# One training step on one core: program order on every engine, transposes moved into the forward part, one pass over w2 saved, output rows in V's space

## The chip, the cores and the metric

The kernel runs on one core of a Trainium2 chip. The metric is the device time of one execution in microseconds (us), lower is better; each time quoted is the median of several executions. An execution over 1.5% above the fastest of its kernel counts as slow. The notes called "the Trainium skill" are cited by page title and section where the argument rests on them.

Names: PE is TensorE (PEld its weight loads), DVE is VectorE, ACT is ScalarE, POOL is GpSimd, SP is SyncE. A tile is a piece of on-chip memory that the program allocates from a pool. PE's results go into tiles in PSUM, and DVE or ACT copy them from there to SBUF; such a copy of an output is called an eviction. A one-bank tile holds 512 values of 4 bytes, or 1024 of 2 bytes, in each partition (row of memory), and a two-bank tile twice that.

## The reference

A step of decoding with its backward pass, batch and sequence length 1, in bfloat16:

```python
x = x + attention(layernorm(x), K, V, wq, wo)   # A1: 32 heads, 4 kv heads of 128, last 4096 of 32768 positions
x = x + mlp(layernorm(x), w1, b1, w2)           # B2: 1024 -> 3584 (mish) -> 1024
x = x + attention(layernorm(x), K, V, wq, wo)   # A3: the same weights again
x = x + mlp(layernorm(x), w1, b1, w2)           # B4: the same weights again
out, vjp = jax.vjp(f, x, K, V, wq, wo, w1, b1, w2)
return out, *vjp(grad_out)
```

Matrices are multiplied with one column only, so every weight is read for one 128x1 product per 128x128 block. The backward needs the weights transposed, in blocks of 128x128, which PE does against an identity. The weight gradients are outer products, and the cache gradients (4 x 32768 x 128 each) are zero outside the last 4096 positions: 112 blocks of 0.5 MB of zeros must be written ("the zeros").

## The kernel before

The kernel streams weights in chunks of 0.5 MB. These are the parts that matter (cuts are marked with `# ...`).

```python
ctx.enter_context(tc.manual_schedule(engines={ET.SP}))  # only SP in program order; the scheduler orders the others
pt   = ctx.enter_context(tc.tile_pool(name="pt", bufs=4, space=PSUM))    # one-bank tiles
pbig = ctx.enter_context(tc.tile_pool(name="pbig", bufs=1, space=PSUM))
pacc = ctx.enter_context(tc.tile_pool(name="pacc", bufs=1, space=PSUM))

def xpose_unit(ap2d, nb):                       # 8 transposes, one PSUM tile of their own, one copy back in place
    ps = pt.tile([P, 8, P], BF16, name="tps", tag="pt")
    for b in range(nb):
        nc.tensor.transpose(ps[:, b, :], ap2d[:, b * P:(b + 1) * P], ident_bf[:])
    evac(ap2d, ps[:, 0:nb, :].rearrange("p b c -> p (b c)"), 0.08 * nb, 0.12 * nb)   # on DVE or ACT by load

# backward of w2, one chunk of 16 blocks (w1 and wo are alike)
    zeros(1)                                    # one 0.5 MB write of zeros beside each chunk
    for tt in range(2):
        xpose_unit(w[:, tt, :], 8)
    for tt in range(2):
        # ... 8 products 128x1 each

def xpose_resident():                           # V, K and wq stay in SBUF; all their transposes in one go, in A3's backward
    xpose_kv(V_t); xpose_kv(K_t)
    # ... wq

# outputs: each weight gradient brings its vectors into rows by small DMAs, then outer products
def rows_put(R, side, kind, groups):
    rt = to_rows(...)                           # one of 4 buffers "rt"
    for q, off, b0, nb, step in groups:
        for lay in range(2):
            nc.gpsimd.dma_start(R[...], rt[...])        # 80 such row copies in the whole kernel, 0.5 to 2 KB each
R = new_rows("R2"); rows_put(...); dw_tall(R, ...)      # w2, then b1, w1, wo, kv, wq in the same way
# ... four outer products of 512 columns into places of one bank (six in rotation), four evictions of 512
nc.gpsimd.dma_start(out_7.rearrange("(c p t) -> p c t", p=P, t=2), db1_bf[:]...)   # b1's gradient, 7 KB in 4-byte pieces
```

## Time and profile before

Three executions gave 726.65 us in the median (723.12 to 728.49).

| | before |
|---|---|
| span of the profiled execution | 723.6 us |
| bytes moved | 197.29 MB, 273 GB/s |
| PE busy | 470.8 us (65%) |
| mean granted clock | 0.569 |

This is the page of the kernel before, its second part: the span in 40 equal slices of 18.1 us. A digit is the busy share in tenths; PEclk is the granted clock in tenths of full speed; DMA is the share of the 16 DMA engines, and GB/s what they moved.

```profile
PE   3564334563367788988987766778675464878364
...
PEclk9985555555565555757965555555555555555555
DMA  8999999449989999994006999999503646567547
GB/s 317 418 415 408 292 335 372 180 160 326 342 283 396 341 364 374 387 301 167 3 3 240 394 218 354 384 339 346 229 3 151 259 166 242 231 269 249 184 169 296
```

DMA is nearly full almost everywhere up to slice 30, with three holes: A3's forward (slices 8 and 9), the resident transposes and A3's attention (slices 19 to 21), and A1's attention (slices 29 and 30). The last ten slices are the outputs, where DMA is about half busy. The clock is at 0.5 for most of the span.

The next view is the table of stretches: window, then busy time and count of instructions of each engine, granted clock, DMA share, GB/s. The windows are the backward of B4's w2, of B4's w1, the resident transposes, and the outputs.

```profile
core 0: us, PE busy (x) PEld busy (x) DVE busy (x) ACT busy (x) POOL busy (x), PEclk, DMA share, GB/s
208.00:248.00 40.00, 31.15 (x441) 27.28 (x441) 12.19 (x20) 11.13 (x11) 0.65 (x1) 0.59 0.95 346
248.00:292.00 44.00, 36.03 (x464) 31.09 (x465) 12.07 (x21) 12.61 (x15) 0.00 (x0) 0.50 1.00 369
330.00:361.40 31.40, 30.70 (x515) 30.61 (x514) 25.82 (x41) 23.70 (x26) 0.00 (x0) 0.92 0.15 55
540.00:723.60 183.60, 108.67 (x517) 36.18 (x516) 97.72 (x171) 90.80 (x166) 86.06 (x159) 0.50 0.58 218
```

The backward of w1 is at DMA share 1.00 although PE is busy for 36 of 44 us at clock 0.50: each 0.5 MB weight chunk carries a 0.5 MB zero write, so it is the transfers that set its pace. From 330 us DMA is nearly idle (share 0.15) while PE transposes, at clock 0.92, and DVE and ACT copy.

These are waits of PE by what ended them: microseconds in total, number of waits, longest. PE waits for copies (the `w_c` lines) when it multiplies with the transposed chunk.

```profile
PE acc L170 <- DMA w_c<-in_B_w_dram: 47.9, 52, 2.0
PE acc L170 <- ACT w_c L150: 20.3, 45, 0.8
...
PE acc L170 <- DVE w_c L147: 7.6, 34, 0.4
...
PE tps L155 <- DMA w_c<-in_B_w_dram: 5.8, 4, 3.8
```

The row copies land 1.5 to 3.4 us after their issue, most kinds at about 1.6. This line is from the list of DMA issues (count, size, median us from issue to landing):

```profile
Ro<-rt POOLq DMA_DIRECT2D x16, 2.0 KB, 1.6
```

### The profile page before, as it was taken

How to read it: one execution, taken by the hardware profiler on the slowest of the kernel's cores; microseconds unless marked ns; L12 is line 12 of the kernel's file. 1: busy time of each engine (PE TensorE's matmuls, PEld its weight loads, DVE VectorE, ACT ScalarE, POOL GpSimd, SP SyncE). 2: the span in 40 equal slices, each digit the busy share in tenths (PEclk: the TensorE clock that was granted, in tenths of full speed). 3: DMA queues.
4: the chain of work that ended last, by engine and by line, in shares of the span. 5: the costliest groups of instructions: out<-in, count | busy, mean ns of one | idle time of the engine just before them, and what ended most of it. 6: DMA issues, size and time to landing. Idle time of an engine off the chain costs nothing. (4 is left out here: it accounts for less than half of the span.)

```text
span 723.6 us, 16229 instructions
## 1 busy us (share of the span) xinstructions
PE 470.8 (65%) x7092; PEld 352.3 (49%) x7092; DVE 236.4 (33%) x468; ACT 199.8 (28%) x294; POOL 89.8 (12%) x173
## 2 busy tenths in 40 slices
PE   3564334563367788988987766778675464878364
PEld 2444334353356676868976655667461010135210
DVE  1140010200122322526823221222314454676255
ACT  0120000000012222425802222222104464665245
POOL 0000000000000000000000000000005555423462
PEclk9985555555565555757965555555555555555555
DMA  8999999449989999994006999999503646567547
GB/s 317 418 415 408 292 335 372 180 160 326 342 283 396 341 364 374 387 301 167 3 3 240 394 218 354 384 339 346 229 3 151 259 166 242 231 269 249 184 169 296
DMA packets 59751, 197.29 MB, mean 273 GB/s; under 512 B 12577, under 2 KB 12577, under 8 KB 58657
## 3 DMA queue, kind: packets, MB, share of 16 engines
q1 hardware_dynamic: 46800, 156.27, 59.7%
q0 software_dynamic: 12880, 40.00, 14.8%
q8 instruction: 55, 0.90, 0.5%
q14 instruction: 16, 0.12, 0.1%
HBM read 97.53 MB, written 98.58 MB: 271 GB/s over the span
## 5 line engine op out<-in xcount | busy, mean ns | idle before, releaser
L170 PEld LDWEIGHTS <-w_c 128*128 128x128 bf16 x1792 | 61.1, 105 | 106.6 <-DMA w_c<-in_B_w_dram 56.2
L150 ACT COPY w_c<-tps 128x1024 bf16<-128x1024 bf16 (+1 forms) x52 | 47.3, 909 | 163.0 <-PE tps L155 89.2
L147 DVE COPY w_c<-tps 128x1024 bf16<-128x1024 bf16 (+1 forms) x68 | 45.8, 677 | 127.0 <-PE tps L163 67.1
L163 PE MATMUL tps<-ident_bf,w_c 128*128 128x128 bf16 x448 | 52.9, 311 | 5.8 <-DMA w_c<-in_B_w_dram 5.8
L155 PE MATMUL tps<-ident_bf,w_c 128*128 128x128 bf16 x448 | 49.2, 296 | 5.8 <-DMA w_c<-in_B_w_dram 5.8
L163 PEld LDWEIGHTS <-w_c 128*128 128x128 bf16 x448 | 45.2, 144 | 5.9 <-DMA w_c<-in_B_w_dram 5.9
L155 PEld LDWEIGHTS <-w_c 128*128 128x128 bf16 x448 | 42.5, 138 | 6.2 <-DMA w_c<-in_B_w_dram 6.1
L155 PE MATMUL tps<-ident_bf,wo_c 128*128 128x128 bf16 x352 | 40.3, 307 | 0.0
L170 PEld LDWEIGHTS <-wo_c 128*128 128x128 bf16 x608 | 20.4, 105 | 36.8 <-DMA wo_c<-in_A_wo_dram 14.0
L155 PEld LDWEIGHTS <-wo_c 128*128 128x128 bf16 x352 | 35.0, 143 | 0.0
L170 PE MATMUL acc<-nB_pair,w_c 128*128 128x1 bf16 x448 | 16.7, 166 | 28.1 <-DMA w_c<-in_B_w_dram 25.0
L150 ACT CAST st_t<-ops 128x512 bf16<-128x512 f32 x43 | 24.2, 597 | 35.9 <-PE ops L170 31.1
L170 PE MATMUL acc<-a_pair,w_c 128*128 128x1 bf16 x448 | 16.2, 166 | 27.4 <-DMA w_c<-in_B_w_dram 23.0
L147 DVE COPY wo_c<-tps 128x1024 bf16<-128x1024 bf16 x26 | 18.0, 691 | 47.9 <-PE tps L155 47.4
L150 ACT COPY wo_c<-tps 128x1024 bf16<-128x1024 bf16 x18 | 18.2, 1012 | 51.6 <-PE tps L155 51.6
L147 DVE CAST st_t<-ops 128x512 bf16<-128x512 f32 x39 | 25.5, 684 | 20.6 <-PE ops L170 18.9
L170 PE MATMUL acc<-dh_pair,w_c 128*128 128x1 bf16 x448 | 21.5, 168 | 16.4 <-ACT w_c L150 11.2
L170 PE MATMUL acc<-gB_pair,w_c 128*128 128x1 bf16 x448 | 19.4, 167 | 12.9 <-ACT w_c L150 9.1
L170 PE MATMUL ops<-Rq 2*128 2x512 bf16 x42 | 17.2, 586 | 14.5 <-DMA Rq<-rt 13.4
L170 PE MATMUL ops<-Ro 2*128 2x512 bf16 x44 | 18.1, 587 | 10.8 <-DMA Ro<-rt 8.4
L170 PE MATMUL acc<-gA_pair,wo_c 128*128 128x1 bf16 x352 | 16.3, 168 | 13.2 <-ACT wo_c L150 10.2
L520 POOL DMA_DIRECT2D out_dram<-rt x2 | 1.2, 588 | 190.8 <-DVE rt L515 190.8
(545 smaller groups left out, 819.7 us busy)
## 6 DMA issues: line engine op xcount, KB each, us to landing
out_dram<-zt SPq DMA_DIRECT2D x112, 512.0 KB, 7.3
w_c<-in_B_w_dram SPq DMA_DIRECT2D x64, 448.0 KB, 5.3
w_c<-in_B_w_dram SPq DMA_DIRECT2D x52, 512.0 KB, 5.6
wo_c<-in_A_wo_dram SPq DMA_DIRECT2D x38, 512.0 KB, 6.6
out_dram<-st_t POOLq DMA_DIRECT2D x30, 512.0 KB, 3.6
out_dram<-st_kv POOLq DMA_DIRECT2D x16, 512.0 KB, 4.8
out_dram<-st_wq POOLq DMA_DIRECT2D x16, 512.0 KB, 3.7
K_163<-in_A_k_cache_dram SPq DMA_DIRECT2D x1, 1024.0 KB, 12.5
```

The source lines that it names most:

```text
L147: nc.vector.tensor_copy(out_ap, in_ap)
L150: nc.scalar.copy(out_ap, in_ap)
L155: nc.tensor.transpose(ps[:, b, :], ap2d[:, b * P:(b + 1) * P], ident_bf[:])
L163: nc.tensor.transpose(ps[:, b, :], ap2d[:, o:o + 2 * P - 1:2], ident_bf[:])
L170: nc.tensor.matmul(out_ap, lhsT=lhsT, rhs=rhs, start=start, stop=stop, skip_group_check=True, **kw)
L520: nc.gpsimd.dma_start(out_flat.rearrange("(n p) -> n p", p=P), rt[0:n, :])
```

## The change

Its intent is to take three holes out of the DMA's work. The resident blocks are transposed in the forward part, where PE has time between loads; B4's last forward pass over w2 also serves its backward, so ten w2 loads and a 40 us stage disappear; and V's space, free after the last attention, holds more output buffers, so that all row copies can be issued together and evictions be 1024 wide. The backward loops are software-pipelined by one chunk, and the order of the program is now the order on every engine. The diff, cut to its core (cuts marked `...`):

```diff
-    ctx.enter_context(tc.manual_schedule(engines={ET.SP}))
+    ctx.enter_context(tc.manual_schedule())
-    pt = ctx.enter_context(tc.tile_pool(name="pt", bufs=4, space=bass.MemoryType.PSUM))
-    pbig = ctx.enter_context(tc.tile_pool(name="pbig", bufs=1, space=bass.MemoryType.PSUM))
+    vpool = tc.alloc_tile_pool(name="vpool", bufs=1)
+    p2 = ctx.enter_context(tc.tile_pool(name="p2", bufs=3, space=bass.MemoryType.PSUM))
...
+    def psum2(shape, dtype, name):                       # a tile of two banks
+        t = p2.tile([P, 1024 if dtype == FP32 else 2048], dtype, name=name, tag="p2")
+        return shaped(t, shape)
+
+    def xpose2(halves):
+        ps = psum2([P, 16, P], BF16, "tps")
+        for i, (blocks, dst) in enumerate(halves):
+            for b, ap in enumerate(blocks):
+                nc.tensor.transpose(ps[:, 8 * i + b, :], ap, ident_bf[:])
+            n = len(blocks)
+            evac(dst, ps[:, 8 * i:8 * i + n, :].rearrange("p b c -> p (b c)"), 0.08 * n + 0.03, 0.11 * n + 0.15)
...
+    def pipe(items, T, M, lag=1):                        # transposes of chunk i, then products of chunk i-1
+        n = len(items)
+        for i in range(n + lag):
+            if i < n:
+                T(items[i])
+            if i >= lag:
+                M(items[i - lag], i - lag)
...
+            if g_bf is not None:                         # B4's w1 forward also transposes resident blocks
+                zeros(i % 2)
+                fill(2 if i % 2 else 1)
...
+            fwd_rows2(yacc, w, c, a_bf, c == 0, c == NW2 - 1)
+            if g_bf is not None:                         # B4's w2 forward also serves the backward
+                ...
+                xpose_rows2(w)
+                if held:
+                    bwd_rows2(dacc, held.pop(), c - 1, g_bf)
+                held.append(w)
...
+    def after_v():                                       # called in A1's backward, V is dead from there
+        vpool.release()
+        ...
+        rows["w2"] = new_rows("R2")
+        rows_put(rows["w2"], 0, "a", tall_groups(TF))
+        ...                                              # all eight row sets, 80 row copies
     zeros(1000)                                          # the 58 zero blocks left, without a wait, on SP
...
-                for q in range(4):
-                    ev_out(sts[q // 2][:, q % 2, i * 512:(i + 1) * 512], pss[q])
+            pss = [psum2([P, 1024], FP32, "ops") for _ in range(2)]
             for i in range(2):
+                for tt in range(2):
+                    b = 2 * c + tt
+                    outer(R, b % 4, (b // 4) * P, i * 512, pss[tt][:, i * 512:(i + 1) * 512])
+            for tt in range(2):
+                ev_out(st[:, tt, :], pss[tt][:])
```

## The prediction

> **What bounds it now.** Timeline and stage windows of the span (723.6 us) show three regimes.
> 1. Forward, 0 to 208 us: A1 and B2 (3 to 121 us) run at DMA share 0.95 to 1.01, 337 to 407 GB/s: bound by loads. A3 (121 to 163) is a latency chain, share 0.54.
> 2. Backward, 208 to 540 us. Streamed stages (208 to 330, 384 to 516) have DMA share 0.94 to 1.01, because each 0.5 MB weight chunk carries a 0.5 MB zero write; a chunk takes about 3.0 us. PE transposes, waits for the copy (0.3 to 0.8 us on ACT or DVE), multiplies; its granted clock is mostly 0.50 and 16 transposes take 1.87 us. From 330.9 to 361.4 PE only transposes resident V, K and wq (warm, 16 in 0.89 us) while DMA moves 55 GB/s; then comes attention (3 GB/s).
> 3. Output, 540 to 724 us: DMA share 0.58. 80 row copies issued by POOL, 0.52 us each, stall every matrix; 512-wide evictions take 0.684 us (DVE) and 0.597 us (ACT); four stage buffers.
>
> **What the change does.**
> - Removes the 30.5 us resident block; its 32 pairs of transposes go to A3's wo loop (8) and B4's w1 loop (24).
> - B4's w2 pass also serves the backward: the 40 us stage at 208 to 248 goes, B4's own w2 loop grows from about 21 to 30-35 us. 10 w2 and 6 wo chunk loads fewer (197 to about 189 MB).
> - Backward loops are pipelined by one chunk: PE no longer waits for copies. I expect the clock to rise to 0.8-1.0 there (dense stretch 294 to 300 us: 1.00). The Trainium skill, "TensorE: Matmul & The Clock Gate", Part 4, says transposes do not raise the clock; this trace disagrees (1.00 from 336 to 340 us, transposes alone).
> - Only about 54 of 112 zeros stay before the tail, 58 follow the last wo load. Backward chunks fall to 1.3-2.0 us.
> - Output: 1024-wide evictions (estimate from the 512-wide ones: 1.22 and 1.03 us, so 1.13 us per engine and chunk instead of 1.28), nine stage buffers, all row copies together (41 us of POOL) ahead of the first output write, partly under A1's backward.
>
> **Sum (end of stage, us).** A1+B2: 115 (was 121). A3: 162. B4 w1 with 24 fills: 198. w2 double pass: 232. w1 backward: 258. wo backward: 286. A3 attention backward: 308 (was 384). B2 w2: 334; w1: 360. A1 wo: 383; attention: 410 (was 540). Tail: row copies hold the first output write until about 450, while the 58 zeros (30 MB, 78 us) drain; then 69 of 78 chunks at about 1.5 us: 555 to 565. DMA alone from about 372 us: 70 MB at 380 GB/s is 185 us, giving 557; both limits agree.
>
> Prediction: 570 us, range 542 to 612. Faster by over 2%: 0.97; within 2%: 0.02; slower: 0.01.
>
> **What would show it.** No PE-only transposes with idle DMA; backward stages of about 25 us with clock over 0.7; first output write about 40 us after the last attention's row transposes begin, zeros filling DMA there; tail DMA share over 0.85; about 189 MB.
>
> **What would make it wrong.** Clock staying 0.50 in backward (up to 50 us more). Row copies holding DVE (four row buffers, eight row sets) and delaying A1's gradient. Three two-bank PSUM buffers limiting output chunks to 1.8 us (20 us more). DMA hiccups as at 430 us (102 GB/s at share 0.91).

## The result, and the profile after

The changed kernel took 796.62 us (795.54 to 797.42, four runs), the kernel before 724.97 us (723.12 to 728.49, four runs): ratio 1.098, 95% interval 1.093 to 1.103. It is slower by 10%, where 570 us was predicted. A ratio here is the mean time of one kernel's fast runs over the mean of the other's fast runs of the same rounds, so it is not quite the ratio of the quoted medians.

The bytes are as predicted, 188.88 MB. This is the same part of the page of the changed kernel; a slice is now 19.9 us.

```profile
PE   2476335676766677777677676777631543466653
...
PEclk9999999655555555555555555555555555555555
DMA  7993999437554376574170356688999498755476
GB/s 236 409 415 144 370 372 399 197 105 258 184 170 134 88 233 195 173 253 175 53 247 21 126 160 197 193 306 278 417 411 413 171 358 230 287 243 185 160 270 258
```

In the backward (slices 14 to 28) PE is at about 0.7 all along and DMA mostly at 0.3 to 0.7, with the clock at 0.5 from slice 9 to the end. Nothing is full, so something makes both wait. The stretches are B4's w1 pass with its 24 fills, the w2 double pass, the backward of w1, the row copies under the zeros, and the outputs:

```profile
core 0: us, PE busy (x) PEld busy (x) DVE busy (x) ACT busy (x) POOL busy (x), PEclk, DMA share, GB/s
184.70:262.00 77.30, 51.41 (x612) 47.17 (x611) 23.08 (x43) 19.85 (x22) 0.00 (x0) 0.50 0.52 171
262.00:313.00 51.00, 38.15 (x670) 35.81 (x671) 12.88 (x23) 11.13 (x11) 0.00 (x0) 0.50 0.56 173
313.00:360.00 47.00, 32.73 (x456) 30.00 (x453) 12.24 (x22) 12.03 (x14) 0.00 (x0) 0.50 0.71 225
560.00:614.00 54.00, 18.96 (x441) 14.47 (x442) 6.82 (x24) 0.98 (x3) 25.44 (x50) 0.50 1.03 414
634.00:795.70 161.70, 80.81 (x471) 29.61 (x466) 80.09 (x82) 76.94 (x74) 46.24 (x81) 0.50 0.71 247
```

The predicted lengths were 36, 34 and 26 us for the first three; they took 77, 51 and 47 us. PE's waits say why (the same columns as before). The transposes, which never waited for a copy before, now do:

```profile
PE tps L153 <- DVE w_c L128: 32.9, 42, 0.8
...
PE tps L153 <- ACT w_c L131: 20.4, 18, 1.1
...
PE tps L153 <- DVE wo_c L128: 7.8, 10, 0.8
...
PE tps L153 <- ACT K_172 L131: 4.4, 4, 1.1
```

Added up over all lines of this kind, this is 111.5 us in 124 waits, one in each pass of 14 or 16 transposes. One pass of the backward of w1 in the timeline of the changed kernel (start, duration, engine, line, what, count; in brackets the idle time before it and what ended it):

```profile
318.98 1.01 PE L153 MATMUL tps<-ident_bf,w_c 128*128 128x128 bf16 x8
...
320.04 0.69 DVE L128 COPY w_c<-tps 128x1024 bf16<-128x1024 bf16 x1 [0.61 <-PE tps L153]
320.78 0.80 PE L153 MATMUL tps<-ident_bf,w_c 128*128 128x128 bf16 x6 [0.78 <-DVE w_c L128]
...
321.38 0.55 PE L171 MATMUL acc<-dh_pair,w_c 128*128 128x1 bf16 x14
...
321.79 1.01 PE L153 MATMUL tps<-ident_bf,w_c 128*128 128x128 bf16 x8
```

PE transposes eight blocks, DVE copies them out for 0.69 us, and only then PE transposes the other six, after an idle time of 0.78 us. The two groups go to different halves of one tile `tps`. When ACT does the copy the idle time is 1.1 us. A chunk takes 2.81 us (from 318.98 to 321.79), of which PE's useful work at this clock is about 2.

The outputs start at 634.6 us. The row copies, which were to take 41 us, now run from 575 to 634 us, because most land later:

```profile
Ro<-rt POOLq DMA_DIRECT2D x16, 2.0 KB, 5.9
```

### The profile page after: what moved, and what is told of

It reads as the page before. It is cut to its first block, busy times and chain, and to the rows that moved or that the text cites. A ratio compares the mean times of both kernels' runs of the same rounds, so it can differ in the third digit from the quotient of the medians.

```text
span 795.7 us, 15860 instructions
## 1 busy us (share of the span) xinstructions
PE 475.2 (60%) x6996; PEld 373.6 (47%) x6996; DVE 227.7 (29%) x388; ACT 192.4 (24%) x208; POOL 91.5 (12%) x174
## 2 busy tenths in 40 slices
DMA packets 57444, 188.88 MB, mean 237 GB/s; under 512 B 12320, under 2 KB 12320, under 8 KB 56352
## 4 chain that ended last, share of the span: by engine, by line
PE 49%; DMA 20%; ACT 15%; DVE 11%; issue 3%; POOL 1%; ACTq 0%; SPq 0%; POOLq 0%; DVEq 0%
PE tps L153 27%; PE acc L171 11%; PE ops L171 8%; DMA w_c<-in_B_w_dram 5%; DVE w_c L128 4%; ACT st_t L131 3%; ACT w_c L131 3%; DMA out_dram<-st_w_8005 2%; DMA R_7435<-rt 2%; ACT st_kv L131 2%; DMA K_176<-in_A_k_cache_dram 2%; ACT st_wq L131 2%; PE big L171 2%; DMA wo_192<-in_A_wo_dram 2%; DMA R_7410<-rt 2%
## 5 line engine op out<-in xcount | busy, mean ns | idle before, releaser
L153 PE MATMUL tps<-ident_bf,w_c 128*128 128x128 bf16 x896 | 114.3, 307 | 53.3 <-DVE w_c L128 32.9
L131 ACT CAST st_t<-ops 128x1024 bf16<-128x1024 f32 x33 | 33.1, 1013 | 69.5 <-PE ops L171 65.0
L153 PE MATMUL tps<-ident_bf,wo_c 128*128 128x128 bf16 x256 | 32.4, 307 | 14.6 <-DVE wo_c L128 7.8
L128 DVE CAST st_t<-ops 128x1024 bf16<-128x1024 f32 x27 | 33.0, 1224 | 26.7 <-PE ops L171 22.5
L153 PEld LDWEIGHTS <-wo_c 128*128 128x128 bf16 x256 | 25.9, 141 | 17.2 <-issue 17.2
L594 POOL DMA_DIRECT2D R_7410<-rt x16 | 8.2, 519 | 158.3 <-DVE rt L572 156.5
L128 DVE CAST st_kv<-ops 128x1024 bf16<-128x1024 f32 x15 | 18.4, 1224 | 27.5 <-PE ops L171 26.1
L171 PE MATMUL ops<-R_7435 2*128 2x512 bf16 x64 | 13.0, 540 | 21.9 <-ACT st_w_8095 L131 3.4
L171 PE MATMUL ops<-R_7410 2*128 2x512 bf16 x56 | 16.5, 600 | 14.8 <-ACT st_t L131 11.1
L131 ACT CAST st_kv<-ops 128x1024 bf16<-128x1024 f32 x17 | 17.1, 1012 | 31.6 <-PE ops L171 30.6
L128 DVE CAST st_wq<-ops 128x1024 bf16<-128x1024 f32 x15 | 18.4, 1225 | 10.2 <-PE ops L171 10.2
```

What stands on the lines that cost most here:

```text
L128: nc.vector.tensor_copy(out_ap, in_ap)
L131: nc.scalar.copy(out_ap, in_ap)
L153: nc.tensor.transpose(ps[:, 8 * i + b, :], ap, ident_bf[:])
L171: nc.tensor.matmul(out_ap, lhsT=lhsT, rhs=rhs, start=start, stop=stop, skip_group_check=True, **kw)
L594: nc.gpsimd.dma_start(R[32 * q + lay:32 * q + lay + 1, side, off:off + nb * P].rearrange("o (n p) -> o n p", p=P), rt[lo:lo + (nb - 1) * s ...
```

## The experiments

Twelve kernels ran. All gave correct results. The table lists them; the ratio is to the kernel before in the same rounds.

| run | what differs | us (median) | ratio, 95% interval |
|---|---|---|---|
| change | | 796.62 | 1.098 (1.093 to 1.103) |
| E1 | change, 16 transposes ahead of both copies | 632.38 | 0.877 (0.871 to 0.883) |
| E2 | change, each half its own PSUM tile | 625.42 | 0.867 (0.864 to 0.871) |
| E3 | change, scheduler on again | 631.53 | 0.878 (0.872 to 0.884) |
| E4 | before, in program order | 748.54 | 1.037 (1.034 to 1.041) |
| E5 | E2, output products tile by tile | 609.68 | 0.842 (0.838 to 0.847) |
| E6 | E2, one-bank tiles in the outputs | 582.60 | 0.802 (0.795 to 0.809) |
| E7 | E2, row copies issued by ACT | 655.13 | 0.907 (0.902 to 0.911) |
| E8 | E6 and E7 | 602.16 | 0.833 (0.829 to 0.837) |
| E9 | E6, row copies between output chunks | 587.34 | 0.814 (0.809 to 0.818) |
| E10 | E6, zeros after the row copies | 640.21 | 0.889 (0.883 to 0.895) |
| E11 | E6, b1's gradient written in rows | 578.12 | 0.799 (0.795 to 0.802) |
| E12 | E9 and E11's write | 584.74 | 0.808 (0.805 to 0.811) |

### E1 to E4: why the backward did not get faster

Theory A: the second half's transposes wait for the copy of the first half because both are in one PSUM tile, and in program order nothing else can go ahead. A rival (A') was that the wait is for the weight tile, which is read and overwritten in place half by half. Another rival was that program order by itself is what costs.

E1 changes the order inside a pass, and keeps the tile:

```diff
         for i, (blocks, dst) in enumerate(halves):
             for b, ap in enumerate(blocks):
                 nc.tensor.transpose(ps[:, 8 * i + b, :], ap, ident_bf[:])
+        for i, (blocks, dst) in enumerate(halves):
             n = len(blocks)
             evac(dst, ps[:, 8 * i:8 * i + n, :].rearrange("p b c -> p (b c)"), ...)
```

> The changed kernel with one edit: all 16 transposes of a pair of halves are issued before the two copies. Theory A (in program order, PE's second eight transposes wait for the copy of the first eight out of the same PSUM tile: 0.78 us on DVE, 1.10 us on ACT, in each of 124 passes, about 115 us in all): those waits vanish and the time falls from 796 to about 680 us if the granted clock stays at 0.50, to about 600 us if the denser PE also warms up. Theory B (giving up the scheduler on the compute engines is what costs, whatever the order inside a pass): under 25 us gained, so above 770 us.

E2 keeps the order, and gives each half a tile:

```diff
-        ps = psum2([P, 16, P], BF16, "tps")
         for i, (blocks, dst) in enumerate(halves):
+            ps = psum2([P, 8, P], BF16, "tps")
             for b, ap in enumerate(blocks):
-                nc.tensor.transpose(ps[:, 8 * i + b, :], ap, ident_bf[:])
+                nc.tensor.transpose(ps[:, b, :], ap, ident_bf[:])
```

> The changed kernel, order kept (eight transposes, copy, eight transposes, copy), but each half gets its own PSUM tile. Theory A in the form that the wait belongs to the shared PSUM tile: most of the waits vanish and it lands within 40 us of the run with all 16 first (three tiles in rotation leave some waits). Theory A' (the wait belongs to the weight tile, into which the first copy writes in place while the next transposes read it): no change, about 796 us.

E3 takes program order away from the changed kernel, and E4 gives it to the kernel before:

```diff
# E3, in the changed kernel
-    ctx.enter_context(tc.manual_schedule())
+    ctx.enter_context(tc.manual_schedule(engines={ET.SP}))
# E4, in the kernel before
-    ctx.enter_context(tc.manual_schedule(engines={ET.SP}))
+    ctx.enter_context(tc.manual_schedule())
```

> The changed kernel with the scheduler given back for PE, DVE, ACT and POOL; only SP stays in program order. Theory B: most of the loss comes back, below 720 us. Theory A alone: the wait of the second half stays but may be filled with other PE work, so 700 to 770 us. Neither: near 796 us.

> The kernel before with program order on all engines and nothing else. It gives each half its own PSUM tile. Theory B: it loses as much as the change did, 40 to 80 us over before. Theory A: it loses little, below 750 us, since its transposes of the second half have no copy to wait for; only the multiplies wait.

Measured: 632.38, 625.42, 631.53 and 748.54 us. E1 lies between its two times (680 us with the clock at 0.50, 600 us with it risen), but does not tell A from A', since with all transposes first neither tile can make one wait. E2 does: its order of instructions and its weight tile are those of the changed kernel; only the place of the second half's result is another one. That alone takes away 171 us (796.62 less 625.42; the ratio to before falls from 1.098 to 0.867). Theory A' falls, since E2 left the weight tile as it was. Program order alone costs 28 us in the kernel before (748.54 less 720.47, the median of before in these rounds); that is under Theory A's 750 us, if only just, and short of Theory B's 40 to 80. Program order together with the shared tile costs 165 us in the changed kernel (796.62 less 631.53): with the same shared tile, but E3's scheduler, the transposes' waits for copies are 22.5 us instead of 111.5. So it is the two together that hurt, and either cure is enough for most of it. E3's time is the one that Theory B expected, but its 165 us are not all from these waits: its first output write came at 500.7 us (634.6 in the changed kernel, 463.2 in E2), and its outputs then took 128 us instead of 161, so the scheduler helped the outputs too.

The waits of E2's transposes, in all:

```profile
PE tps L153 <- DMA w_c<-in_B_w_dram: 14.3, 17, 1.4
...
PE tps L153 <- DMA wo_c<-in_A_wo_dram: 5.1, 6, 1.9
...
PE tps L153 <- DMA K<-in_A_k_cache_dram: 3.1, 1, 3.1
...
PE tps L153 <- ACT K L131: 0.6, 3, 0.2
...
PE tps L153 <- ACT V L131: 0.4, 2, 0.2
```

The transposes' waits for copies are down from 111.5 us to 1.0 (0.6 for K's, 0.4 for V's). What remains is waits for loads, as before the change. The stretches of E2 that answer to those of the changed kernel, in the same order:

```profile
164.60:200.40 35.80, 30.98 (x611) 30.42 (x612) 22.48 (x43) 19.38 (x22) 0.00 (x0) 0.88 0.99 369
200.40:230.60 30.20, 28.45 (x673) 27.91 (x673) 12.66 (x24) 11.13 (x11) 0.00 (x0) 0.83 0.81 293
230.60:260.70 30.10, 24.69 (x453) 23.91 (x449) 12.40 (x24) 12.03 (x14) 0.00 (x0) 0.77 0.96 324
388.00:463.00 75.00, 31.20 (x481) 16.22 (x482) 16.67 (x32) 11.00 (x13) 41.40 (x81) 0.50 0.96 383
463.00:624.20 161.20, 80.09 (x467) 29.52 (x466) 80.11 (x82) 76.94 (x74) 45.83 (x80) 0.50 0.71 248
```

They take 35.8, 30.2 and 30.1 us, where 36, 34 and 26 were predicted, at DMA shares of 0.99, 0.81 and 0.96 and clocks of 0.77 to 0.88. The clock is the second half of the loss. PE was busy for 475.2 us in the changed kernel and 387.4 us in E2 with the same work, 87.8 us less, with the clock higher. One transpose took 314 ns in the median before the cure and 219 ns after it. The waits and the slower clock add up to more than 171 us (110.5 and 87.8); part is taken back, E2's transposes waiting for loads instead (the first line above and its like).

The idle times were short, 0.78 to 1.14 us in these passes and none above 1.57 us from 262 to 560 us, and PE was still busy for 70% of the backward of w1 (32.73 of 47 us in the window from 313 us). The Trainium skill, "TensorE: Matmul & The Clock Gate", section "Why this matters for your kernels", gives idle times above about 3 us as what drops the clock. Here the clock stayed at 0.50 for 300 us (from 262 to 560 us) with much shorter ones only. The same page's section "A second HAM failure mode: psum-queue depth-cycling" says that micro-idles between groups of matmuls make the clock oscillate. In the changed kernel's trace there was no oscillation; in E2's the clock went to and fro between 0.50 and 1.00 in the backward.

That the clock rose when the waits were removed is shown by E1 and E2. What decides it is not: neither the length of the idle times nor the busy share puts the cases in order. In the backward of w1, the kernel before had no idle time above 0.51 us and PE busy for 36.03 of 44 us (82%), at clock 0.50; E1 had idle times up to 0.97 us and PE busy for 19.27 of 25.3 us (76%), at clock 1.00.

Does the hardware demand such a wait? The Trainium skill, "PSUM — Partial Sum Buffer", section "PSUM bank collisions raise a hardware error", says that two engines must be kept apart by bank and quadrant. Each half of `tps` is 8 x 128 values of 2 bytes, 2 KB in a partition, which is one bank on that page. So the page's rule does not ask for the wait between the halves; the program's own dependency tracking set it. That it treats a PSUM tile as a whole can be read in the kept traces: in E1 the two copies out of one tile never ran at once (0 of the 48 passes over `w_c` in which DVE and ACT shared them), though they read different halves; in E2, from two tiles, they did in 49 of 50. E2 transposes into one tile while another is copied, and is correct, so nothing seen here contradicts the page.

### E5 and E6: the outputs

E2's forward and backward are within a few microseconds of the prediction: attention's backward ended near 403 us (410 predicted). But its outputs took from 463 to 624 us instead of from 450 to 560. Theory T1: a chunk needs two of three two-bank tiles, its products are issued alternately into both, so both copies start after the last product and PE waits for a copy in each chunk. Rivals: T2, DMA bandwidth; T3, the row copies alone.

E5 makes a tile complete before the next begins:

```diff
-            for i in range(2):
-                for tt in range(2):
+            for tt in range(2):
+                for i in range(2):
...
-            for q in (0, 2, 1, 3):          # w1 and wq
+            for q in (0, 1, 2, 3):
```

> E5 is E2 (two PSUM tiles per 16 transposes, 625 us) with the output matmuls issued tile by tile, so that a two-bank tile is finished and its copy can start before the other tile's matmuls begin; kv chunks unchanged. Theory T1 (the output chunks are held by the release of the three two-bank PSUM tiles): chunks of w2, w1, wo and wq fall from about 2.0 to about 1.5 to 1.6 us, total 590 to 605 us. Rival T2 (DMA bandwidth holds the output part, its share being .54 to .86 there): chunks stay near 2.0 us, total 618 to 628 us. Rival T3 (the row copies decide, the tail being late only because it starts late): total 620 to 628, first output write still at 463 us, chunk period unchanged.

E6 gives the transposes' tiles back before the outputs and takes six one-bank tiles:

```diff
+    p2.release()
+    one["pool"] = ctx.enter_context(tc.tile_pool(name="p1", bufs=6, space=bass.MemoryType.PSUM))
...
-            pss = [psum2([P, 1024], FP32, "ops") for _ in range(2)]
+            pss = [psum1([P, 512], FP32, "ops") for _ in range(4)]
...
-        evac(out_ap, in_ap, 1.22, 1.05)
+        evac(out_ap, in_ap, 0.70, 0.62)
```

> E6 is E2 with the transpose PSUM tiles given back before the output part and six one-bank tiles there, with 512-wide evictions (0.68 us VectorE, 0.60 us ScalarE each in the trace of before). T1: chunks about 1.3 to 1.5 us, kv about 2.3 us, total 575 to 592 us; the output part from first write to end about 115 us instead of 161. T2 (DMA): no better than 618 us. T3: 620 to 628 us. First output write stays at about 463 us under all three.

Measured: 609.68 and 582.60 us. The first output write stayed at 464.2 and 463.4 us. From the first and last issue of wq's 16 blocks, a chunk took 1.77 us in E2 (592.3 to 618.8), 1.27 in E5 (581.1 to 600.1) and 1.30 in E6 (551.1 to 570.6); a kv chunk 2.85, 2.85 and 1.51 us. So T1 holds, E5's total falling a little short of what T1 expected (590 to 605). T2 and T3 fall as the main cause. The 1024-wide eviction itself took what was estimated (1.22 us on DVE, 1.01 on ACT), and E5 keeps it, so for wq it was the order of the products that cost. For kv, whose order E5 left alone, E6 brought the gain; it changes the width and the number of the tiles (three of two banks, six of one) at once, and no run separates the two. E2's and E6's stretches of kv and wq outputs:

```profile
560.00:600.00 40.00, 24.36 (x184) 13.36 (x181) 19.32 (x23) 16.78 (x17) 10.99 (x17) 0.50 0.61 209
```

```profile
520.00:560.00 40.00, 36.37 (x303) 21.64 (x301) 34.93 (x67) 30.43 (x57) 17.37 (x28) 0.50 0.98 368
```

DMA share rose from 0.61 to 0.98 and ACT's and DVE's busy time from 16.78 and 19.32 to 30.43 and 34.93 us of 40. From here on bytes bind E6's outputs.

### E7 to E10: the row copies

Between 403 and 463 us E2's chain of waits consists of row copies. POOL issues six or eight, then waits for one of its four buffers, which comes free when an earlier copy lands. The timeline of E2 shows it:

```profile
403.05 4.11 POOL L594 DMA_DIRECT2D R<-rt  x8 [108.70 <-DVE rt L572]
...
408.41 4.08 POOL L594 DMA_DIRECT2D R<-rt  x8 [1.25 <-DMA R<-rt]
411.74 0.22 DVE L572 COPY rt<-rw 64x128 bf16<-64x128 bf16 x1 [8.42 <-DMA R<-rt]
...
413.92 3.41 POOL L594 DMA_DIRECT2D R<-rt  x6 [1.43 <-DMA R<-rt]
```

T3 was that POOL's issuing holds the start; E7 has ACT issue the same copies, and E8 adds E6.

```diff
-                nc.gpsimd.dma_start(R[...], rt[...])
+                nc.scalar.dma_start(R[...], rt[...])
```

> E7 is E2 with the row copies issued from ScalarE's queue instead of GpSimd's, with the same four buffers. T3 (GpSimd, which takes 60 us for 80 row copies, holds the start of the output part): first output write 20 to 40 us earlier than 463 us, total 590 to 610 us. If the row copies wait for the DMA engines, filled by the zeros (share 1.03), rather than for GpSimd: first output write moves less than 10 us and the total stays 615 to 630 us. T1 and T2 predict no change of the chunk period of about 2.0 us.

> E8 is E6 and E7 together. If both the chunk period and the start of the output part are separate losses, the gains add: 545 to 570 us, the time that the prediction named. If they are one loss (DMA bandwidth), the gains do not add and the total is not below the better of E6 and E7 by more than 5 us.

Measured: 655.13 and 602.16 us, both slower than without it; neither theory had named that. In E7 the 80 copies took ACT 65.8 us to issue, where they took POOL 41.5 in E2. ACT needs longer to issue one: 0.84 us in the median with the zeros running beside it and 0.59 us without, against 0.52 us on POOL. The first write moved 20 us later (483.1 and 484.7 us). The expectation of E8 falls with it: 545 to 570 us was expected. Its other arm (not below the better of E6 and E7) is met in number only, since E7 brought no gain that could be added. The two changes are both seen in it, one with its gain, one with its loss. The Trainium skill, "DMA: Bandwidth & Descriptors", section "Issuing engine by pattern", calls issuing from SP or ACT generally faster than from GpSimd. For the time that the issuing engine spends on these row copies of 0.5 to 2 KB the trace disagrees; when ACT's copies landed, E7's trace does not show.

E10 moves the 58 zero blocks (57 by its trace) from beside the row copies into the outputs:

```diff
-    zeros(1000)
...
+        if stg[0] > 1:
+            zeros(1)                    # one after each output block, issued by POOL
```

> E10 is E6 with the 58 zero blocks that the change lets run beside the row copies moved into the output part, one after each output block, issued by GpSimd. Theory (the zeros filling the DMA queues lengthen each row copy's landing from 1.6 us in the kernel before to 5 to 6 us): landings fall to about 1.5 to 2 us, the row part from about 60 to about 41 us, and the first output write comes at 440 to 447 us instead of 463. The bytes of the zeros must then pass later: 585 to 615 us, no better than E6. If landings stay above 4 us, the zeros are not what lengthens them, and the first write stays at 455 us or later.

Measured: landings of 1.5 to 2.0 us, row copies from 398.7 to 439.5 us (40.8 us), first write at 440.0 us. So the zeros are what lengthens the landings, from 1.5 to 2.0 us here to 3.9 to 6.1 us in E6 (medians of the kinds of copy). The page of E10 has these lines:

```profile
out_dram<-zt POOLq DMA_DIRECT2D x57, 512.0 KB, 10.5
...
Ro<-rt POOLq DMA_DIRECT2D x16, 2.0 KB, 1.6
```

The total is 640.21 us, worse than the expected 585 to 615: DMA moved 4 to 5 GB/s for 42 us from 388 us, and these zeros had to pass later, at share 1.0.

E9 keeps the zeros where they are, and puts six of the eight row sets between the output chunks of w2:

```diff
         rows_put(rows["w2"], 0, "a", tall_groups(TF))
         rows_put(rows["w2"], 1, "gB", rep_groups)
-        ...                                  # the other six sets
...
             nc.gpsimd.dma_start(out_v[c], st[:])
+            if c % 2:
+                next(between, None)          # one of the other six sets
```

> E9 is E6 with the first two of the eight row sets put out where they were and the other six put between the output chunks of w2. In E2 and E6 the chain of waits from 403 to 463 us is row copies, GpSimd waiting each time 4 to 6 us for a landing. Theory T4 (the tail starts late because all row copies stand ahead of the first output write in program order): first output write at 420 to 432 us instead of 463. From 388 us on, E6 moved about 68 MB; at the 0.41 MB per us that the full queues carried, that is 166 us, so 554 us is the floor; total 555 to 570 us. Rival T5 (the row copies were hidden behind the zeros' transfers anyway, so that DMA bytes alone set the end): total within 5 us of E6's 583, only the first write earlier.

Measured: the first write came at 419.7 us, 44 us earlier, and the total is 587.34 us, within 5 us of E6's 582.60. T4 falls and the number is T5's: an early start is worth nothing here. T5's reason, that bytes alone set the end, holds only in part. The output blocks, the row copies and the zeros share full queues up to 450 us (share 1.03), but from 450 to 490 us the share was 0.66 while POOL still issued row copies, which delays the blocks behind them.

### E11 and E12: a 7 KB write

In E6 the queues were slow from 480 to 495 us. The bias gradient is written in 1792 pieces of 4 bytes, and took 19.8 us from issue (475.5 us) to landing. E11 and E12 transpose it on PE first, and write 14 rows of 512 bytes.

```diff
-    nc.gpsimd.dma_start(out_7.rearrange("(c p t) -> p c t", p=P, t=2), db1_bf[:]...)
+    dbp = psum2([NW2, 2, P], BF16, "dbp")
+    for tt in range(2):
+        nc.tensor.transpose(dbp[:, tt, :], db1_bf[:, tt::2], ident_bf[:])
+    db_row = stage_tile([NW2, P, 2], "db_row")
+    nc.vector.tensor_copy(db_row[:].rearrange("c p t -> c t p"), dbp)
+    nc.gpsimd.dma_start(out_7.rearrange("(c q) -> c q", q=2 * P), db_row[:].rearrange("c p t -> c (p t)"))
```

> E11 is E6 with the 7 KB bias gradient transposed on TensorE first, so that it is written in 14 pieces of 512 bytes instead of 1792 pieces of 4 bytes. In E6 that write took 19.8 us to land, and from 480 to 495 us the queues were at share 1.43, 0.85 and 0.80 with 321, 28 and 171 GB/s. Theory T6 (the write of 4-byte pieces blocks the output blocks behind it): the landing falls under 6 us, no stretch of low rate at high share remains after 470 us, total 565 to 575 us instead of 583. Rival: the low rate comes from the other output writes (strided rows of 3.5 KB): rate unchanged there, total 578 to 586 us.

> E12 is E9 with the same write in rows. In E9 the row copies between the output chunks brought the first output write from 463 to 420 us and the total not down. T6: what E9 won was lost behind the 4-byte pieces and the wait for stage buffers at 470 to 490 us (share .42), and comes out now: 555 to 570 us, 5 us or more below E11. Rival T5 (the first write's time does not matter because GpSimd issues row copies and output blocks in one order): E12 within 5 us of E11, or above it.

Measured: 578.12 and 584.74 us. The stretches of E6 and then of E11:

```profile
480.00:485.00 5.00, 3.77 (x12) 0.90 (x12) 2.94 (x5) 3.12 (x7) 1.63 (x3) 0.50 1.43 321
485.00:490.00 5.00, 1.18 (x4) 0.30 (x4) 1.33 (x2) 1.03 (x2) 0.54 (x1) 0.50 0.85 28
490.00:495.00 5.00, 1.19 (x4) 0.21 (x4) 1.05 (x2) 1.32 (x2) 0.54 (x1) 0.50 0.80 171
```

```profile
480.00:485.00 5.00, 4.26 (x16) 0.83 (x14) 3.61 (x7) 4.65 (x9) 2.20 (x4) 0.50 1.03 396
485.00:490.00 5.00, 4.10 (x15) 1.00 (x13) 4.01 (x7) 3.94 (x9) 1.63 (x3) 0.50 1.04 395
490.00:495.00 5.00, 4.96 (x20) 0.94 (x19) 4.45 (x10) 5.00 (x10) 2.55 (x5) 0.50 1.00 380
```

The slow stretch is gone, 28 and 171 GB/s having become 395 and 380, and w1's 16 blocks were issued in 19.4 us instead of 28.0. E9 and E12 differ in the same way: from 490 to 500 us E9's queues moved 86 and 82 GB/s, E12's 278 and 371. As to the transfer rate T6 is confirmed. The kernel before had the same write, from 421.6 to 437.6 us, and its queues moved 138 and 102 GB/s from 425 to 435 us: this is the place of the "DMA hiccups as at 430 us" that the prediction named without a cause. As to the total it is not shown: E11 lies 4.5 us below E6, their intervals (0.795 to 0.802 and 0.795 to 0.809) overlap, and 565 to 575 us was expected. The landing of the write took 9.8 us in E11, not under 6, and 3.5 us in E12 (12.2 in E9). E12 is above E11, by 6.6 us and with separate intervals, so E12's rival T5 stands.

The Trainium skill, "DMA: Bandwidth & Descriptors", section "Rules for kernel authors", says that a last dimension that is not contiguous becomes one descriptor per element, and to rearrange it. The case here is near to that but not the same: the last dimension is contiguous, and only two elements (4 bytes) long. The cure was of the same kind, with the numbers above.

E11 has the lowest ratio measured, though it is not separated from E6: 0.799 of the time before, and 0.727 of the changed kernel's (0.7987 over 1.0981).

## Why the prediction was wrong

- **The step that failed** is the third bullet, "Backward loops are pipelined by one chunk: PE no longer waits for copies." The pipelining removed the products' wait for copies, but the transposes got one of their own: each pass puts two halves into one tile, with the first half's copy between them in program order. This was 111.5 us of waits, and it undid the rest of that bullet, the clock's rise: 0.50 instead of the "0.8-1.0" expected. E2 shows both, 171 us in one change of allocation. The text listed "Clock staying 0.50 in backward (up to 50 us more)" as a risk, without a cause for it. Its size was near: for the same 3525 PE instructions of the backward stages PE was busy for 223.2 us in the changed kernel (262 to 575 us) and 166.9 in E2 (200.4 to 403 us), 56.3 us apart. The waits came on top of it.
- **The sum over stages was right once that step is repaired.** E2's stages ended at 116, 165, 200, 231, 261, 288, 311, 337, 365 and 388 us, where 115, 162, 198, 232, 258, 286, 308, 334, 360 and 383 were written. So the values of removing the resident block, the w2 pass and the zeros in the backward were right, with 188.88 MB as predicted, and the clock in E2's streamed backward stages was 0.77 to 0.94 except 0.70 in the last.
- **The outputs were mis-sized**, and this is independent of the first step. "69 of 78 chunks at about 1.5 us" was about 2 us in E2 (463 to 624 us, 161 us, over 78 chunks). The named risk, "Three two-bank PSUM buffers limiting output chunks to 1.8 us (20 us more)", came true with twice the size: E6's tiles gave 43 us (625.42 to 582.60), of which E5's order alone gave 16. "Tail DMA share over 0.85" was 0.71 in E2, and 0.98 in E6's stretch from 520 us.
- **The row copies** were to hold the first output write "until about 450". Their POOL time was right, 41 us. The zeros placed over them stretched the landings, which added 60 less 41 us, about 19; the first write came at 463 us in E2. E9 shows that this cost next to nothing by the time that bytes bind the outputs.
- **The clock remark about transposes** was right in the trace of before, and again in E2: the granted clock was 0.77 to 0.94 in the streamed stages where transposes are most of PE's work (0.70 in the last).

What stays open: why the changed kernel's clock stayed at 0.50 with 70% busy PE (no run varied the idle time by itself), whether the width or the number of PSUM tiles made kv faster in E6, and how much of E11's gain over E6 is real.

## What to carry to other kernels

When a scheduler is replaced by program order, look for waits that it was filling: two groups of work in one tile, with a copy of the first between them, are a chain, though the halves are disjoint. Split the tile, or issue all producers first. The same holds for PSUM tiles in an output loop: the copy of one tile must be able to overlap the products of the next. Finish one tile before the next is begun (E5), or have more tiles (E6). And starting something earlier is worth only what the resource that binds afterwards still has to give.

## What the Trainium skill lacked or had wrong

- "TensorE: Matmul & The Clock Gate", Part 4, says that transposes do not raise the clock. In the trace of before, PE did transposes alone from 330.9 us, the clock rose from 0.50 to 1.00 at 334.9 us, and was 1.00 from 336 to 340 us; in E2 a transpose took 219 ns in the median against 314 ns at clock 0.50.
- The same page, "Why this matters for your kernels", gives only idle times above about 3 us as what drops the clock (the page names micro-idles elsewhere, without a length). With none above 1.57 us the clock stayed at 0.50 from 262 to 560 us. When the transposes' waits for copies were removed (E2), it was 0.77 to 0.94 in most of the streamed backward stages. Idle length alone does not decide it: E1 had clock 1.00 with idle times up to 0.97 us, the kernel before 0.50 with none above 0.51 us.
- "PSUM — Partial Sum Buffer" has the hardware's rule of bank and quadrant; no page says that a program's waits can follow the allocated tile instead, as E1 and E2 show here. This cost 111.5 us of direct waits and 171 us in all here.
- "DMA: Bandwidth & Descriptors", "Issuing engine by pattern", calls SP and ACT the faster issuers. To issue one small row copy took ACT 0.59 us, or 0.84 us while SP issued zeros, and GpSimd 0.52 us (E7 and E2).
- No page gives the landing of a small copy behind large writes of the same core: medians of 1.5 to 2.0 us (E10) became 3.9 to 6.1 us (E6) while the queues were full (share 1.03).
- "DMA: Bandwidth & Descriptors", "Rules for kernel authors", tells to keep the last dimension contiguous, without a number for what a write of tiny pieces does to the transfers beside it: 7 KB in 4-byte pieces took 19.8 us to land (E6; 12.2 in E9), and for 10 us the queues moved 28 and 171 GB/s where they moved 395 and 380 without it (E11).
